# A recurrence and a routed mixture of experts in one kernel: another list of expert visits, other homes for the first raw weights, and new numbers in the planner

## The chip, the cores and the metric

The kernel runs on one core of one Trainium2 chip. The metric is device time in microseconds (us) of the slowest core, here of the only one. Three timed runs of the kernel before gave a median of 621.38 us (621.37 to 622.74). One more execution, of 622.83 us, was profiled; every row below is from it.

## The reference

A gated recurrence runs over 4 sequences of 5056 steps with 256 channels. Its 20,224 result rows go through a router: a row whose skip score is not positive is passed on as it is, every other row goes to one of 8 experts, a two-layer network with a hidden width of 1024.

```python
f = lower_bound + (1 - lower_bound) * sigmoid(f_logit)
for t in range(S):
    h = f[:, t] * h + (1 - f[:, t]) * x[:, t];  y[:, t] = h
x = y.reshape(B * S, D)
do = x @ w_skip > 0
logits = x[do] @ w_gate;  e_idx = argmax(logits);  gate_w = softmax(logits)[e_idx]
out[do] = x[do] + gate_w * (relu(x[do] @ w1[e_idx]) @ w2[e_idx])      # the other rows: out = x
```

With the inputs of the reference the experts 0 to 7 get 1150, 1630, 1047, 1244, 1259, 1255, 1392 and 937 rows; the other 10,310 are passed on.

## The kernel before, in words

The sequence is cut into 20 chunks (19 of 256 steps, one of 192), each worth 8 tiles of 128 rows (the last 6). A chunk is loaded by ACT's queue (`load_z`, `load_x`), goes through `tanh` and `affine` on ACT, `mixin` and eight `scan` instructions on DVE, is transposed to rows by PE (`turn_out`) and copied by ACT (`evict`). PE multiplies it with the router's weights (`score`), and DVE works out for each row the expert and a place in that expert's region of a table in memory (`route0` to `route3`, the last of which writes `posi`; `gates`). GpSimd then writes the rows to their places with one indirect DMA per tile (`send`, L485), 8 to a chunk.

The experts' work is done in visits. A visit (e, ns, m) takes ns tiles of expert e out of the table once the chunks up to m are in it. The list VISITS (L57) has 22 of them with 72 tiles. `window` (DVE) sets where a visit reads: at the next unread row, or, where the region does not yet hold ns tiles more, further back, so that it ends at the last row there; the rows read twice are masked. `fetch` (SP) loads the rows, `turn_in` (PE) transposes them, `x_hi` and `x_lo` (ACT, DVE) split them into two parts, PE does the first layer as three products (`first`, L610), ACT and DVE rectify and split the hidden values (`rect_hi`, `rect_lo`), PE does the second layer (`second`, L653), DVE weighs the result (`weigh`, L658), and GpSimd writes one tile per indirect DMA to the output (`put_out`, L662). Weights come half an expert at a time by SP (`load_w`, L534) into raw buffers and are split by ACT and DVE (`split_hi`, `split_lo`). The first three visits use raw weights in plain float32, without splits.

What the list does not cover is worked out on the chip when all chunks are routed (`list1` to `list4`): windows of 2 tiles and of 3 tiles. One of the former and two of the latter (SURE) are part of the program as three more visits with the expert in a register. If there are more, a loop at the program's end does them one after the other (L960 to L990); every engine reads the count `more` and branches over the loop if it is zero.

The order of the instructions on each engine is fixed before the program runs, by a planner (`Plan.run`): each job has a cost, a due time, jobs that it needs and slots that it takes from rings which stand for buffers; an engine takes the first job by due time that can start in the planner's account. MOVES shifts due times by name, chunk and visit. The chip then runs each engine's queue in that order, and an instruction at its head that waits holds up all behind it.

`hold` (L538) gives a raw weight its buffer ahead of the load, by a memset of one element on DVE; the memset waits until the readers of what was there before are done. The raw weights of the first three visits have the tags `w1h` and `w2h`, three buffers each.

Of the kernel before, what the change touches and what calls it, by code (L numbers as in the profile page):

```python
# [40 lines left out]
NEAR, FAR, TURN = 0.2, 1.1, 140.0  # L41
MOVES = {
    ("tanh", "early"): 4.3, ("evict", "early"): -2.8, ("send", "early"): -1.8, ("load_x", "chunk", 2): -8.4,
    ("gates", "chunk", 3): 3.1, ("scan", "chunk", 4): -4.5, ("score", "chunk", 4): 1.4, ("scan", "chunk", 5): 2.8,
    ("turn_out", "chunk", 5): -3.2, ("route1", "chunk", 5): 3.2, ("score", "chunk", 6): 1.3,
    ("affine", "chunk", 7): 8.9, ("scan", "chunk", 7): 2.6, ("route3", "chunk", 7): -5.7, ("chunk", 8): -4.1,
    ("scan", "late"): -5.1, ("score", "late"): 0.3, ("score_turn", "late"): -3.0, ("turn_out", "late"): 5.7,
    ("route0", "late"): -10.1, ("chunk", 11): -0.7, ("chunk", 15): -2.3, ("chunk", 16): -1.8,
    ("hold", "early"): 2.5, ("pass_over", "visit", 0): -3.8, ("put_out", "early"): 10.4, ("hold", "visit", 1): -5.6,
    ("rect_all", "visit", 1): -16.1, ("split_lo", "early"): -0.6, ("turn_in", "visit", 3): 4.2,  # L50
    ("first", "visit", 3): 2.0, ("rect_hi", "early"): 4.0, ("split_lo", "visit", 4): -5.3,
    ("split_lo", "visit", 5): -1.0, ("x_lo", "visit", 5): -6.8, ("window", "visit", 6): -11.7,
    ("x_lo", "visit", 6): -10.7, ("rect_lo", "late"): 1.4, ("rect_lo", "visit", 6): -6.9,
    ("second", "visit", 6): 5.5, ("weigh", "visit", 6): 0.4, ("visit", 7): 4.1,
# [198 lines left out]
def hgrn_moe(ctx, tc, z_d, x_d, lb_d, wr_d, w1_d, w2_d, out_d, disp_d):  # L253
# [518 lines left out]
    for n, v in enumerate(visits):  # L772
# [94 lines left out]
    for v, t in zip(visits, begin):  # L867
# [160 lines left out]
```

## Time and profile before

| | us |
|---|---|
| median of three timed runs | 621.38 |
| the profiled execution | 622.83 |
| its span, first to last instruction | 621.1 |
| PE busy in the span | 571.6 (92%) |
| DVE busy | 490.2 (79%) |
| ACT busy | 348.2 (56%) |
| POOL busy | 284.9 (46%) |

A row of the timeline has the start, the duration, the engine (SPq is SP's queue, which issues DMAs; PEld the loading of weights), the line of the kernel, the operation, the tiles written and read, and in brackets how long the engine had been idle before and what ended that. Starts of neighbours tell more than durations: the durations of instructions that follow each other overlap.

### The profile page before, as it was taken

What the parts mean: (1) busy time and instruction counts of PE and PEld (TensorE: products, weight loads), DVE (VectorE), ACT (ScalarE), POOL (GpSimd) and SP (SyncE); (2) the same over time, 40 slices, a digit from 0 to 9 for tenths busy, and PEclk for the clock granted to TensorE, in tenths of its full rate; (3) what the DMA queues carried; (4) which work ended last, traced back from release to release, by engine and by line L of the source; (5) the groups of instructions that cost most, each with busy time, mean ns of one, the idle gap of its engine ahead of it and who ended that gap; (6) DMA issues with size and microseconds to landing.
All of it is one profiled execution on the core that took longest, in us unless ns stands there. A gap on an engine that the chain in (4) does not pass through costs nothing.

```text
span 621.1 us, 11689 instructions
## 1 busy us (share of the span) xinstructions
PE 571.6 (92%) x4012; PEld 513.2 (83%) x4012; DVE 490.2 (79%) x1131; ACT 348.2 (56%) x518; POOL 284.9 (46%) x297
## 2 busy tenths in 40 slices
PE   2648999996999999999999999999999999999981
PEld 1327888996899988989898899889999999999971
DVE  5997999896999999999999998567964567466351
ACT  5865687873784856677666544535443445354140
POOL 2278677876027374563788556274320322022201
PEclk9767999997999999999999999999999999999976
DMA  8898999987786697796988755564543417444100
GB/s 319 343 394 323 400 415 411 349 281 284 260 333 246 249 377 291 276 311 253 345 320 292 244 175 181 163 225 178 197 145 128 130 37 247 130 149 148 59 5 24
DMA packets 40431, 149.64 MB, mean 241 GB/s; under 512 B 9332, under 2 KB 10507, under 8 KB 33328
## 3 DMA queue, kind: packets, MB, share of 16 engines
q1 hardware_dynamic: 22544, 86.91, 39.8%
q10 hardware_dynamic: 6304, 41.42, 17.9%
q0 software_dynamic: 11520, 20.52, 8.9%
q8 instruction: 33, 0.54, 0.3%
q14 instruction: 30, 0.25, 0.1%
HBM read 106.79 MB, written 53.23 MB: 258 GB/s over the span
## 4 chain that ended last, share of the span: by engine, by line
PE 67%; DMA 12%; ACT 1%; DVE 1%; issue 1%; POOL 1%; POOLq 0%; SPq 0%; DVEq 0%
PE po L653 30%; PE ph L610 29%; DMA out<-xin 8%; PE pt L403 3%; PE px L560 3%; PE pq L381 2%; DMA rw<-w 2%; DMA xin<-dispatched 1%; DMA dispatched<-rows,posi 1%; POOL dispatched L485 1%; PE pl L395 0%; DVE hl L629 0%; ACT hh L617 0%; ACT w2h L548 0%; ACT zt L356 0%
## 5 line engine op out<-in xcount | busy, mean ns | idle before, releaser
L485 POOL DMA_INDIRECT dispatched<-rows,posi x158 | 179.9, 1139 | 156.7 <-issue 36.1
L617 ACT ACTIVATE hh<-ph 128x512 fp32r<-128x512 f32 (+1 forms) x164 | 93.3, 572 | 159.4 <-PE ph L610 138.2
L653 PE MATMUL po<-w2h,hh 128*128 128x256 f32 x616 | 177.8, 289 | 0.0
L653 PE MATMUL po<-w2l,hh 128*128 128x256 f32 x616 | 175.1, 284 | 0.4 <-DVE w2l L553 0.4
L653 PE MATMUL po<-w2h,hl 128*128 128x256 f32 x616 | 172.7, 280 | 0.4 <-DVE hl L629 0.2
L662 POOL DMA_INDIRECT out<-xin x82 | 90.9, 1108 | 173.9 <-DVE xin L658 136.7
L629 DVE SCALAR_TENSOR_TENSOR hl<-ph,hh 128x512 fp32r<-128x512 f32 (+1 forms) x164 | 105.8, 650 | 63.9 <-ACT hh L617 63.0
L610 PE MATMUL ph<-xh,w1h 128*128 128x512 f32 (+2 forms) x368 | 133.9, 364 | 1.2 <-ACT w1h L548 1.2
L610 PE MATMUL ph<-xh,w1l 128*128 128x512 f32 (+2 forms) x368 | 132.4, 360 | 1.8 <-DVE w1l L553 1.8
L610 PE MATMUL ph<-xl,w1h 128*128 128x512 f32 (+2 forms) x368 | 132.6, 360 | 0.0
L653 PEld LDWEIGHTS po<-w2h,hh 128*128 128x128 f32 x616 | 116.5, 189 | 4.7 <-issue 2.1
L653 PEld LDWEIGHTS po<-w2h,hl 128*128 128x128 f32 x616 | 116.5, 189 | 2.9 <-DVE hl L629 1.0
L653 PEld LDWEIGHTS po<-w2l,hh 128*128 128x128 f32 x616 | 116.2, 189 | 0.6 <-DVE w2l L553 0.6
L373 DVE TENSOR_TENSOR_SCAN xt<-zt,xt 128x256 f32<-128x256 f32 (+1 forms) x160 | 108.7, 722 | 3.8 <-issue 3.2
L610 PEld LDWEIGHTS ph<-xl,w1h 128*128 128x128 f32 x368 | 70.6, 192 | 8.8
L610 PEld LDWEIGHTS ph<-xh,w1h 128*128 128x128 f32 x368 | 70.2, 191 | 8.9 <-issue 2.1
L610 PEld LDWEIGHTS ph<-xh,w1l 128*128 128x128 f32 x368 | 70.5, 192 | 7.7 <-DVE w1l L553 2.0
L403 PE MATMUL pt<-ident,xt 128*128 128x128 f32 x316 | 50.7, 295 | 16.8 <-DVE xt L373 15.5
L548 ACT ACTIVATE w2h<-rw 128x1024 fp32r<-128x1024 f32 x46 | 48.7, 1060 | 29.4 <-PE po L653 24.4
L553 DVE TENSOR_TENSOR w2l<-rw,w2h 128x1024 fp32r<-128x1024 f32 x46 | 55.9, 1215 | 7.8 <-ACT w2h L548 7.6
L403 PEld LDWEIGHTS pt<-ident,xt 128*128 128x128 f32 x316 | 39.0, 149 | 26.4 <-issue 12.9
L553 DVE TENSOR_TENSOR w1l<-rw,w1h 128x1024 fp32r<-128x1024 f32 x46 | 55.9, 1218 | 3.4 <-ACT w1h L548 3.3
(126 smaller groups left out, 629.9 us busy)
## 6 DMA issues: line engine op xcount, KB each, us to landing
rw<-w SPq DMA_DIRECT2D x92, 512.0 KB, 4.8
out<-rows SPq DMA_DIRECT2D x19, 1032.0 KB, 10.0
zt<-z ACTq DMA_DIRECT2D x18, 1024.0 KB, 9.1
xt<-x ACTq DMA_DIRECT2D x18, 1024.0 KB, 5.2
xin<-dispatched SPq DMA_DIRECT2D x13, 516.0 KB, 5.3
w1f<-w SPq DMA_DIRECT2D x6, 512.0 KB, 8.4
w2f<-w SPq DMA_DIRECT2D x6, 512.0 KB, 10.0
dispatched<-rows,posi POOLq DMA_INDIRECT x158, 6.1
```

What stands on the lines that cost most here:

```text
L373: V.tensor_tensor_scan(out=xt[:, k, sl], data0=zt[:, k, sl], data1=xt[:, k, sl], initial=first_h, op0=ALU.mult, op1=ALU.subtract)
L381: T.matmul(pq[g * GR:(g + 1) * GR], wq[:, k], xt[:, k, 2 * P * g:2 * P * (g + 1)], start=(k == 0), stop=(k == KD - 1))
L403: T.transpose(pt[:, s_, k * P:(k + 1) * P], xt[:, k, (2 * g + s_) * P:(2 * g + s_ + 1) * P], ident)
L485: si = G.indirect_dma_start(out=disp_d, out_offset=bass.IndirectOffsetOnAxis(ap=posi[:, j:j + 1], axis=0), in_=rows[:, j], in_offset=None, ...
L548: A.activation(hi, v["raw"][h, nm], AF.Copy)
L553: V.tensor_tensor(out=lo, in0=v["raw"][h, nm], in1=v["w"][nm, h][0], op=ALU.subtract)
L560: T.transpose(px[:, s_ * P:(s_ + 1) * P], xin[:, s_, k * P:(k + 1) * P], ident)
L610: T.matmul(ph[:, i], a[:, k, cs], b[:, k, :w], start=(n == 0), stop=(n == 5))
L617: A.activation(th, v["hid"][u], AF.Relu)
L629: V.scalar_tensor_tensor(out=tl, in0=ph, scalar=0.0, in1=th, op0=ALU.max, op1=ALU.subtract)
L653: T.matmul(v["po"][p][:, q], a[:, i, cs], b[:, c], start=(fb == 0 and n == 0 and q == 0), stop=(fb == NFB - 1 and n == len(pairs) - 1), sk ...
L662: oi = G.indirect_dma_start(out=out_d, out_offset=bass.IndirectOffsetOnAxis(ap=v["ids"][:, s, D:D + 1], axis=0), in_=v["xin"][:, s], in_of ...
```

## The change

The list has the same 22 visits' worth of tiles in another order: (0, 3, 8) becomes (0, 3, 10) and goes two visits later, (3, 4, 11) becomes (3, 4, 13), (4, 4, 18) becomes (4, 4, 17), (0, 4, 17) becomes (0, 4, 19). The raw weights of the three first visits go to three tags, `r{}` with 2 buffers, `{}l` and `{}h` with 3 each. The planner's costs change (`send` 1.28 to 1.42, `put_out` 1.36 to 1.42, among others), a ring for `sq` and an order among takers of `{}l` are added, and MOVES is replaced by a longer table. The memory's zeroed margin (`clear`) now waits for a memset on DVE.

```diff
-NEAR, FAR, TURN = 0.2, 1.1, 140.0
+NEAR, FAR, TURN = 0.1, 0.8, 140.0
 MOVES = {
-    ("tanh", "early"): 4.3, ("evict", "early"): -2.8, ("send", "early"): -1.8, ("load_x", "chunk", 2): -8.4,
...
+    ("load_z", "early"): 5.7, ("load_x", "chunk", 0): 10.5, ("affine", "early"): 14.3, ("scan", "chunk", 0): -12.3,
...
-VISITS = [(3, 1, 0), (2, 2, 1), (1, 2, 2), (0, 2, 3), (3, 2, 4), (5, 2, 5), (6, 4, 7), (0, 3, 8), (1, 3, 8), (4, 4, 9), (7, 4, 10), (3, 4, 11), (5, 4, 12), (6, 4, 13), (1, 4, 15), (2, 4, 16), (0, 4, 17), (4, 4, 18), (5, 4, 19), (1, 4, 19), (3, 3, 19), (7, 4, 19)]
+VISITS = [(3, 1, 0), (2, 2, 1), (1, 2, 2), (0, 2, 3), (3, 2, 4), (5, 2, 5), (6, 4, 7), (1, 3, 8), (4, 4, 9), (7, 4, 10), (0, 3, 10), (5, 4, 12), (3, 4, 13), (6, 4, 13), (1, 4, 15), (2, 4, 16), (4, 4, 17), (5, 4, 19), (0, 4, 19), (1, 4, 19), (3, 3, 19), (7, 4, 19)]
...
+    def late_clear():
+        V.memset(zero[0:1, 0:1], 0.0)
...
+    HOMES = (("r{}", 2), ("{}l", 3), ("{}h", 3))
...
         if v["whole"]:
-            r = sb.tile(shp, F32, name=nm + "f", tag=nm + "h", bufs=3)
+            tag, n = HOMES[v["i"] % 3]
+            r = sb.tile(shp, F32, name=nm + "f", tag=tag.format(nm), bufs=n)
...
-            J["clear"] = job("SP", 1.3, ready[0], clear, need=[J["scan", 0][0, 0]], kb=760)
+            n_ = job("DVE", .07, ready[0] - 18, late_clear, need=[J["scan", 0][1, 0]])
+            J["clear"] = job("SP", 1.3, ready[0] - 18, clear, need=[n_], kb=760)
...
-        s1 = job("ACT", .32, r - 20.2, score_out, c, need=[s0], uses=[s_p])
-        s2 = job("PE", .24, r - 20.2, score_turn, c, need=[s1], takes=[s_l])
+        s_q = new_slot("sq")
+        s1 = job("ACT", .32, r - 20.2, score_out, c, need=[s0], takes=[s_q], uses=[s_p])
+        s2 = job("PE", .24, r - 20.2, score_turn, c, need=[s1], takes=[s_l], uses=[s_q])
...
-        J["send", c] = [job("POOL", 1.28, r - 11 + j * 1.2, send, c, j, need=[r3, ga, nu], uses=[s_r, s_o], kb=74, lands=2.8)
+        J["send", c] = [job("POOL", 1.42, r - 11 + j * 1.2, send, c, j, need=[r3, ga, nu], uses=[s_r, s_o], kb=74, lands=2.8)
...
-                s_raw = new_slot(nm + "h") if whole else new_slot("r" + nm)
+                own = HOMES[v["i"] % 3][0].format(nm) if whole else "r" + nm
+                s_raw = new_slot(own)
...
-                lo = job("DVE", 1.21, use - 4, split_lo, v, h, nm, need=[hi], takes=[s_lo], uses=[s_raw, s_hi])
+                lo = job("DVE", 1.21, use - 4, split_lo, v, h, nm, need=[hi], takes=[s_lo], uses=[s_raw, s_hi],
+                         after=taker.get(nm + "l"))
+                taker[nm + "l"] = lo
...
-            job("POOL", 1.36, end + 1 + s_, put_out, v, s_, need=[ob] + [J["keep", c] for c in range(m + 1)],
+            job("POOL", 1.42, end + 1 + s_, put_out, v, s_, need=[ob] + [J["keep", c] for c in range(m + 1)],
```

The places where the order moves are shown as the compiled programs have them, with the lines of each kernel (L543 before is L577 after, L485 is L517, L662 is L696).

DVE around the first `mixin` of chunk 4 (`xt_471`), before; `w1f_629` is the fourth raw first-layer weight and takes the buffer of the first one, `w1f_245`, which visit 0 reads:

```order
L506 TENSOR_SCALAR mask_all_173<-seqf2_157,end_594 128x2
L508 TENSOR_SCALAR place_92<-end_594 128x1
L364 SCALAR_TENSOR_TENSOR xt_471<-zt_349,xt_471 128x1024
L543 MEMSET w1f_629 1x1
L373 SCALAR_TENSOR_TENSOR xt_471<-zt_349,xt_342,xt_471 128x256 x4
```

The same place after, where chunk 4 is `xt_462`; `w1f_589` and `w1f_591` are visit 2's, in buffers that nothing has used before:

```order
L541 TENSOR_SCALAR place_92<-end_568 128x1
L577 MEMSET w1f_589 1x1
L577 MEMSET w1f_591 1x1
L577 MEMSET w2f_594 1x1
L396 SCALAR_TENSOR_TENSOR xt_462<-zt_363,xt_462 128x1024 x2
```

The memsets stand at the same place, and what they wait for is no longer there.

GpSimd up to the writes of chunk 7, before (`rows_976` is chunk 5, `rows_1166` chunk 6, `rows_1326` chunk 7):

```order
L662 DMA out<-xin_617 20224x258
L476 COPY rows_976<-idv_130 128x8
L662 DMA out<-xin_617 20224x258
L485 DMA dispatched<-rows_976,posi_1145 165888x258 x7
L476 COPY rows_1166<-idv_130 128x8
L485 DMA dispatched<-rows_976,posi_1145 165888x258
L485 DMA dispatched<-rows_1166,posi_1280 165888x258 x7
L476 COPY rows_1326<-idv_130 128x8
L485 DMA dispatched<-rows_1166,posi_1280 165888x258
L662 DMA out<-xin_769 20224x258 x2
L485 DMA dispatched<-rows_1326,posi_1523 165888x258 x8
```

And after (`rows_950` is chunk 5, `rows_1082` chunk 6, `rows_1395` chunk 7, `xin_674` visit 1, `xin_854` visit 2):

```order
L517 DMA dispatched<-rows_950,posi_1030 165888x258
L696 DMA out<-xin_674 20224x258 x2
L517 DMA dispatched<-rows_950,posi_1030 165888x258 x2
L508 COPY rows_1082<-idv_130 128x8
L517 DMA dispatched<-rows_950,posi_1030 165888x258 x5
L517 DMA dispatched<-rows_1082,posi_1279 165888x258 x6
L508 COPY rows_1395<-idv_130 128x8
L517 DMA dispatched<-rows_1082,posi_1279 165888x258 x2
L517 DMA dispatched<-rows_1395,posi_1510 165888x258 x8
L696 DMA out<-xin_854 20224x258 x2
```

Two output writes (visit 2's) that stood ahead of chunk 7's stand behind them now: three are ahead in all, where there were five.

GpSimd's last rows are the same in both but for the line numbers; here they are after. The second write of the last visit that is not in a loop stands behind the end of both loops:

```order
L1002 ISA
L1002 UNCONDITIONAL_BRANCH
L999 UNCONDITIONAL_BRANCH
L999 ISA
L999 UNCONDITIONAL_BRANCH
L696 DMA out<-xin_7367 20224x258
L1056 UNCONDITIONAL_BRANCH
```

L1002 is the loop over windows of 3 tiles, L999 the branch around both loops, L1056 the end.

Farther on, the two orders are compared at the thirteenth visit, (5, 4, 12) before and (3, 4, 13) after, which both lists have behind 33 tiles. What stands ahead of its first `x_lo` on DVE, and ahead of its first first-layer product on PE, counted in the compiled programs (kinds that are not named stand there equally often, but for a few of under 0.1 us):

| engine, kind | before | after |
|---|---|---|
| DVE `mixin` | 32 | 33 |
| DVE `scan` | 127 | 128 |
| DVE chunks through `route0` to `gates` | 14 | 15 |
| DVE `split_lo` | 38 | 41 |
| PE transposes of `turn_out` | 224 | 240 |

## Rows read from the trace of the kernel before

**Rows 1.** The page's first part: busy time, share of the span and instructions of each engine.

```profile
PE 571.6 (92%) x4012; PEld 513.2 (83%) x4012; DVE 490.2 (79%) x1131; ACT 348.2 (56%) x518; POOL 284.9 (46%) x297
```

**Rows 2.** The engines' busy time in five stretches of the span; behind each stretch its length, then busy us and instructions of PE, PEld, DVE, ACT and POOL, the granted PE clock, the DMA engines' share and GB/s.

```profile
50.00:140.00 90.00, 89.28 (x668) 79.23 (x667) 81.29 (x207) 68.52 (x104) 67.23 (x64) 0.98 0.95 363
140.00:150.00 10.00, 5.02 (x30) 4.85 (x28) 4.22 (x10) 3.09 (x4) 5.97 (x7) 0.66 0.80 319
150.00:376.00 226.00, 226.00 (x1627) 203.34 (x1626) 217.70 (x453) 145.98 (x218) 121.00 (x107) 1.00 0.78 279
376.00:590.00 214.00, 214.00 (x1484) 199.22 (x1482) 135.77 (x303) 91.79 (x142) 64.31 (x62) 1.00 0.46 153
590.00:621.10 31.10, 15.22 (x97) 14.36 (x96) 9.59 (x16) 6.69 (x10) 2.92 (x3) 0.71 0.04 14
```

**Rows 3.** The last output writes on POOL (timeline), and ahead of them from DVE's timeline the last two weighings of the list's and the SURE visits.

```profile
588.22 0.48 DVE L658 SCALAR_TENSOR_TENSOR xin<-po,xin 128x256 f32<-128x256 f32 x1 [2.89 <-PE po L653]
589.64 0.48 DVE L658 SCALAR_TENSOR_TENSOR xin<-po,xin 128x256 f32<-128x256 f32 x1 [0.93 <-PE po L653]
...
588.98 0.97 POOL L662 DMA_INDIRECT out<-xin  x1 [3.34 <-DVE xin L658]
609.12 0.97 POOL L662 DMA_INDIRECT out<-xin  x1 [19.16 <-DVE xin L658]
...
616.41 0.97 POOL L662 DMA_INDIRECT out<-xin  x1 [5.04 <-issue]
```

**Rows 4.** The page's group of the output writes: count, busy us, mean ns of one, idle us ahead of them by releaser.

```profile
L662 POOL DMA_INDIRECT out<-xin x82 | 90.9, 1108 | 173.9 <-DVE xin L658 136.7 <-issue 20.3 <-DVE place L508 12.1
```

**Rows 5.** The sequencers' instructions of L961 (the branch on `more`) and L964 (the branch on one loop's count: taken into the loop of 2-tile windows first, around the loop of 3-tile windows then): count, shortest, median and longest in ns, start of the first and of the last.

```profile
L961 POOLq COMPARE_BRANCH  x2: 38/39/40, 589.3 to 615.4; - x2
...
L964 PEldq COMPARE_BRANCH  x2: 65/2050/4036, 588.5 to 614.7; - x2
L964 POOLq COMPARE_BRANCH  x2: 34/48/63, 589.8 to 614.4; - x2
...
L964 POOLq INC_SWDGE_SEM  x1: 733/733/733, 614.6 to 614.6; - x1
```

**Rows 6.** Timelines of SP's queue at the start (the zeroed margin, the first weights), and of DVE, PE and SP's queue around 50 us.

```profile
5.96 0.35 SPq L347 DMA_DIRECT2D dispatched<-zero  x1
17.64 9.24 SPq L534 DMA_DIRECT2D w1f<-w  x3
...
49.42 1.22 DVE L364 SCALAR_TENSOR_TENSOR xt<-zt,xt 128x1024 f32<-128x1024 f32 x1
53.85 0.75 DVE L373 TENSOR_TENSOR_SCAN xt<-zt,xt 128x256 f32<-128x256 f32 x1 [3.21 <-issue]
53.86 0.06 DVE L543 MEMSET w1f<- 1x1 f32 x1
...
50.18 3.62 PE L604 MATMUL ph<-xf,w1f 128*128 128x128 f32 x16
...
53.95 0.33 SPq L534 DMA_DIRECT2D w1f<-w  x1
```

**Rows 7.** Timelines of POOL, SP's queue, PE and DVE around the seventh visit, (6, 4, 7): the second of the two output writes ahead of chunk 7, the first and the last of that chunk's eight writes into the table, the visit's fetch, its transposes (PE's row before and some after), its first `x_lo`.

```profile
119.21 0.97 POOL L662 DMA_INDIRECT out<-xin  x1 [0.30 <-DVE place L508]
120.49 0.98 POOL L485 DMA_INDIRECT dispatched<-rows,posi  x1 [0.31 <-issue]
...
131.31 0.97 POOL L485 DMA_INDIRECT dispatched<-rows,posi  x1 [0.31 <-issue]
...
136.51 0.34 SPq L518 DMA_DIRECT2D xin<-dispatched  x1
...
140.20 0.28 PE L653 MATMUL po<-w2l,hh 128*128 128x256 f32 x1
145.46 1.94 PE L560 MATMUL px<-ident,xin 128*128 128x128 f32 x8 [4.98 <-DMA xin<-dispatched]
...
147.21 0.69 DVE L579 TENSOR_TENSOR xl<-px,xh 128x512 fp32r<-128x512 f32 x1 [5.33 <-ACT xh L573]
```

**Rows 8.** What one instruction takes where several of a kind follow each other (a merged row: start, total, count): DVE's `scan`, `mixin` and `split_lo`; the first and the last rows of `route0` with `route1`, and of `route3` with `gates`, of chunk 6; twelve transposes of PE as the chain of waits has them.

```profile
34.38 3.27 DVE L373 TENSOR_TENSOR_SCAN xt<-zt,xt 128x256 f32<-128x256 f32 x5
38.26 2.35 DVE L364 SCALAR_TENSOR_TENSOR xt<-zt,xt 128x1024 f32<-128x1024 f32 x2
148.67 2.35 DVE L553 TENSOR_TENSOR w1l<-rw,w1h 128x1024 fp32r<-128x1024 f32 x2
97.53 0.23 DVE L417 TENSOR_REDUCE mx<-pl 128x8 f32<-128x64 f32 x1 [0.30 <-PE pl L395]
99.01 0.31 DVE L441 TENSOR_TENSOR_SCAN pf<-reset,M 128x72 bf16<-128x72 f32 x1
100.54 0.14 DVE L456 TENSOR_TENSOR base<-carr,pr 128x9 f32<-128x9 f32 x1
101.91 0.20 DVE L472 RECIPROCAL rows<-sm 128x8 f32<-128x8 f32 x1
...
447.02 1.31 PE px L560 x12
```

**Rows 9.** Timelines of DVE and PE at the thirteenth visit: its second `x_lo`, and its first first-layer product.

```profile
294.50 0.66 DVE L579 TENSOR_TENSOR xl<-px,xh 128x512 fp32r<-128x512 f32 x1
...
296.92 0.39 PE L610 MATMUL ph<-xh,w1h 128*128 128x512 f32 x1
```

More of the change, by code (lines that the diff above doesn't have):

```diff
@@ L40 @@
 T0, FETCH, LAG = 55.0, 22.0, 3
-NEAR, FAR, TURN = 0.2, 1.1, 140.0
+NEAR, FAR, TURN = 0.1, 0.8, 140.0
 MOVES = {
-    ("tanh", "early"): 4.3, ("evict", "early"): -2.8, ("send", "early"): -1.8, ("load_x", "chunk", 2): -8.4,
[L44 to L54, printed above, removed]
@@ new lines @@
+    ("load_z", "early"): 5.7, ("load_x", "chunk", 0): 10.5, ("affine", "early"): 14.3, ("scan", "chunk", 0): -12.3,
+    ("turn_out", "early"): 1.9, ("route0", "chunk", 0): -22.6, ("route1", "chunk", 0): -12.6,
+    ("route2", "early"): -2.3, ("route3", "early"): -11.2, ("gates", "early"): 4.0, ("number", "early"): -5.1,
+    ("send", "early"): -3.5, ("chunk", 1): 6.8, ("load_x", "chunk", 1): 11.3, ("mixin", "chunk", 1): 18.5,
+    ("scan", "chunk", 1): -11.8, ("turn_out", "chunk", 1): -21.6, ("evict", "chunk", 1): -27.4,
@@ new lines @@
+    ("scan", "chunk", 8): -9.9, ("score_turn", "chunk", 8): -26.4, ("turn_out", "chunk", 8): 6.2,
+    ("route2", "chunk", 8): 6.9, ("send", "late"): 11.1, ("chunk", 9): -1.1, ("mixin", "late"): 7.3,
+    ("affine", "late"): 7.4, ("scan", "late"): 7.7, ("score", "late"): -5.2, ("score_turn", "late"): -2.5,
+    ("turn_out", "late"): -0.9, ("evict", "late"): 5.3, ("route0", "late"): 8.8, ("exps", "late"): 14.2,
+    ("route2", "late"): -4.0, ("route3", "late"): 7.5, ("load_z", "late"): 1.4, ("chunk", 10): 4.8,
@@ new lines @@
+    ("load_x", "late"): 19.5, ("chunk", 11): 5.9, ("chunk", 12): -14.8, ("chunk", 13): 3.2, ("chunk", 15): 8.4,
+    ("chunk", 16): -10.0, ("chunk", 19): 2.4, ("window", "early"): 3.9, ("visit", 0): 2.9,
+    ("window", "visit", 0): 7.4, ("hold", "early"): 7.2, ("turn_in", "early"): 12.0, ("x_all", "early"): -12.5,
+    ("first", "early"): -10.0, ("rect_all", "early"): 13.8, ("rect_all", "visit", 0): 12.0,
+    ("second", "early"): 6.6, ("pass_over", "early"): 10.9, ("visit", 1): -2.3, ("window", "visit", 1): 6.9,
@@ new lines @@
+    ("first", "visit", 1): -20.2, ("rect_all", "visit", 1): -9.8, ("visit", 2): 2.8, ("window", "visit", 2): 1.7,
+    ("hold", "visit", 2): -9.8, ("first", "visit", 2): 36.0, ("second", "visit", 2): -3.8,
+    ("pass_over", "visit", 2): 15.7, ("put_out", "visit", 2): 8.8, ("visit", 3): 2.3, ("hold", "visit", 3): 7.4,
+    ("split_hi", "visit", 3): 26.4, ("split_lo", "visit", 3): -6.1, ("first", "visit", 3): 10.1,
+    ("rect_hi", "early"): 13.3, ("rect_lo", "early"): -4.7, ("second", "visit", 3): 12.4,
@@ new lines @@
+    ("pass_over", "visit", 3): 5.6, ("visit", 4): 13.0, ("hold", "visit", 4): 10.2, ("split_hi", "visit", 4): -18.8,
+    ("split_lo", "visit", 4): 7.9, ("turn_in", "visit", 4): -9.5, ("x_hi", "visit", 4): 21.5,
+    ("rect_lo", "visit", 4): 13.1, ("second", "visit", 4): 10.3, ("pass_over", "visit", 4): -27.1,
+    ("visit", 5): 4.6, ("split_lo", "visit", 5): 4.3, ("rect_lo", "visit", 5): -5.6, ("second", "late"): 4.7,
+    ("weigh", "late"): -46.8, ("visit", 6): 7.9, ("split_lo", "visit", 6): -23.5, ("split_hi", "late"): -15.6,
@@ new lines @@
+    ("split_lo", "late"): -5.7, ("turn_in", "visit", 6): -7.7, ("first", "late"): 2.0, ("first", "visit", 6): -8.4,
+    ("rect_hi", "late"): 6.9, ("rect_lo", "late"): 7.6, ("rect_lo", "visit", 6): -7.0, ("second", "visit", 6): -5.3,
+    ("window", "late"): 18.0, ("turn_in", "late"): 0.5, ("x_lo", "late"): 7.0, ("visit", 8): 2.9,
+    ("visit", 9): -5.0, ("visit", 11): -1.9, ("visit", 12): 2.0, ("visit", 13): 7.1, ("visit", 14): 2.2,
+    ("visit", 15): -4.9, ("visit", 16): -9.0, ("visit", 18): 0.9, ("visit", 19): -4.4, ("visit", 20): -6.8,
@@ L55 @@
+    ("visit", 21): -9.4, ("visit", 23): 10.0, ("visit", 24): 23.1,
 }
```

19 lines of the change are left out of this document (14 added, 5 removed).

## The prediction

> **What bounds the kernel now.** I read the stretches of the span first, then the end, then the waits of PE and DVE ahead of 150 us. PE is busy for 92% of the span [rows 1]. By stretches, it is never idle from 150 to 590 us, at the full granted clock; DVE is busy for 217.7 of 226 us up to 376, and for 135.8 of 214 behind that [rows 2]. So from 150 to 590 there is no idle time to take out: PE's own work is the length of that stretch, and up to 376 us DVE is close behind it. Time can be won at the two ends, and lost where DVE, which has little to spare up to 376, is asked for something sooner.
>
> At the end the last weighing outside a loop starts at 589.64 and takes 0.48, which is 590.12; the write that belongs to it starts at 616.41, and between the two stand the two writes of a loop's pass [rows 3]. The output writes number 82 [rows 4], while the list has 72 tiles and the SURE visits 8: the loop did one window of 2 tiles. In that stretch PE is busy for half the time at a granted clock of 0.71 [rows 2], because one visit alone has nothing to overlap with.
>
> At the start two waits stand out. DVE sits idle for 3.21 us ahead of 53.85 with "issue" as releaser; right there its queue has the memset of `w1f_629`, which takes the buffer that visit 0 is reading, and PE's products of visit 0 run from 50.18 to 53.80; the load behind that memset is issued at 53.95 [rows 6]. And visit 6 comes too soon for its rows: PE idles 4.98 us and DVE 5.33 [rows 7].
>
> **Part 1, the list.** A visit takes rows from the next unread one, so what is left can be counted from the reference's inputs. Before, expert 0 has 261 rows by chunk 3 and 256 are read. At chunk 8 it has 502, so (0, 3, 8) must step back by 138 to find 3 tiles. With 4 tiles more 1014 of its 1150 rows are read, and 136 rows, two tiles, are left. Expert 2 leaves 347, expert 4 235, expert 6 368: two windows of 2 and two of 3, one more of 2 than SURE has. After, (0, 3, 10) finds 708 rows and steps back by nothing, (0, 4, 19) ends with the last row, and nothing is left of expert 0. The rest is one window of 2 and two of 3, what SURE covers: 80 tiles and no pass of a loop. Experts 3 and 5, whose visits move too, are read to their last row in both.
>
> The price: GpSimd branches around both loops instead of into one. Before, it read the count early and branched at 589.3 [rows 5]. What then stands between it and the last write is what stood there when it branched around the second loop: branch at 614.4, a semaphore step of 0.73, write at 616.41, 2.0 us in all [rows 3, 5]. So the write starts at 589.3 + 2.0 = 591.3, later than the 590.12 of its data. From 616.41 to 591.3 is 25.1 us. What follows that write, 621.1 - 616.41 = 4.7 us, stays.
>
> A long branch can cost more: PE's, around the body of the second loop, took 4036 ns against 65 for the one that fell into the first, and GpSimd's never more than 63 [rows 5]. The Trainium skill (Runtime: NRT & Kernel Launch, section Instruction fetch mechanics) says that a taken branch whose target lies outside the instructions fetched ahead stalls until they are fetched. PE's row agrees with it, and GpSimd's row shows that its code around one loop is short enough; by the page GpSimd might stall around both. PE branches at 588.5 [rows 5] and with 4.04 is through near 592.5, ahead of the end at 596, so that is covered. For GpSimd I take nothing, and keep 4.04 as the upper bound.
>
> **Part 2, the homes.** The first three visits' raw weights no longer share three buffers, and the memsets ahead of chunk 4 take buffers that nothing has used. The 3.21 us go. Not all of it need come through: bounds 0 and 3.2; I take 3.2, since no other reader stands there. Visit 2's four loads can be issued some us sooner, in a stretch where the DMA engines are busy 95% [rows 2]; that is the bound below: a chunk's loads pushed back by 1.5 MB at 363 GB/s, 4 us, if nothing of it were hidden.
>
> **Part 3, visit 6.** Its fetch starts at 136.51, after chunk 7's writes; those start at 120.49, right behind two output writes. In the new order these stand behind chunk 7. From one write's start to the next is 1.28 (119.21 to 120.49), so chunk 7 can be in the table 2.6 us sooner and the rows at 142.7 instead of 145.3. PE was ready for them at 140.5, so some 2 us of its wait stay. Behind the long wait the granted clock was 0.66 [rows 2], the lower of its two levels for a time, and eight transposes took 1.94 us where twelve take 1.31 at the full clock [rows 7, 8]: 1.1 us more than they need. Behind 50 to 140 us of short waits it was 0.98 [rows 2], so I let the shorter wait keep the full clock. DVE's wait shrinks by 2.6 + 1.1 = 3.7. Bounds: 0, and 5.3.
>
> **Part 4, the price in the middle.** The new list wants chunks sooner, and DVE has to make them ahead of the same visits. At the thirteenth visit, behind 33 tiles in both, DVE has done one chunk and three splits more, and one scan: `mixin` 2.35/2 = 1.2; routing 99.01 + 0.31 - 97.53 and 101.91 + 0.20 - 100.54, 3.4; `scan` 3.27/5 = 0.65; three `split_lo` at 2.35/2, 3.5 [rows 8]; 8.8 in all. PE has 16 transposes more, 16 x 1.31/12 = 1.7 [rows 8]. Before, `x_lo` ended at 295.16 and its visit began at 296.92: 1.8 to spare [rows 9]. So DVE is late by 8.8 - 1.7 - 1.8 = 5.3 if it recovers nothing. It recovers 3.2 (part 2) and 3.7 (part 3), together 6.9: the visit can begin 1.6 us sooner than before, and no more, whatever PE gained. PE then has the same tiles left as before, and DVE has room from 376 us on [rows 2]. So the part ahead of the loop ends 1.6 us sooner.
>
> **The rest.** The zeros for the table's margin go out after four scans of chunk 0, near 12 us instead of 5.96; SP's next are the weights at 17.64 [rows 6], so nothing is queued behind them, and the table is read tens of us later. The load order z, z, x, x changes which half comes second; the first `mixin` needs a z half through ACT anyway. The ring for `sq` and the takers change order only. Nothing for these; 1 us either way.
>
> **Sum.** 25.1 + 1.6 = 26.7 off the profiled execution's 622.83 (span 621.1 and 1.7 around it), 596.1. That execution lies 1.45 above the median of 621.38; on the median's scale 594.7 us.
>
> **Rivals.**
> (a) DVE recovers nothing: the waits it loses come back elsewhere, as other waits at its queue's head. For it: DVE is busy 81 of 90 us from 50 to 140 and DMA 95% [rows 2]. Against: the wait at 53.85 had a cause that is removed. Time: 621.4 - 25.1 + 5.3 = 601.6.
> (b) GpSimd's branch stalls like PE's: 594.7 + 4.0 = 598.7. Against it the 63 ns of its own branch.
> (c) Better than forecast: visit 6 waits for nothing, its slow clock goes, and DVE's counts do not bind because it loses less in small waits than before: PE's 4.98 and 1.1 for the 1.6, so 594.7 + 1.6 - 6.1 = 590.2.
> (d) The loop still runs, so that the change does not do what it says: 621.4 - 1.6 = 619.8. For it only a miscount; the 82 writes bear out the same count before.
> (e) Slower than before: rows come late for many visits. Visits 7 to 15 now want their chunk's writes with DVE and GpSimd some us from the edge. If each waited as visit 6 did, 4.98 for the rows and 1.1 at the slow clock, 6.1 per visit; five such visits eat the 26.7 and it is slower from there, and all nine give 594.7 + 55 = 650. For it: the counts of part 4 are tight, and an order that is good in an account can be bad on the chip. Against: before, only visit 6 waited so; PE has no gap behind it until 590 [rows 2].
>
> **How the numbers follow.** Forecast, with its own range of 590 to 600, 0.55; (a) 0.16; (b) 0.08; (c) 0.10; (d) 0.03; (e) or some of its waits without the whole 0.08, half of it over 621. The range that holds the time 8 times in 10 is 588.5 to 604. A difference under 0.3% (1.9 us) can't be told from none: faster 0.94, same 0.02, slower 0.04.
>
> **What would show it.** Output writes number 80, and no row of a loop's body is there; the last write starts within 2 us of its weighing. DVE's idle time ahead of chunk 4's scans is gone. Visit 6's transposes wait under 2 us for rows. At the thirteenth visit `x_lo` ends less than a us ahead of PE's first product, or PE waits for it. I am wrong in part 4 if PE idles over 5 us in all between 150 and 590, in part 1 if the last write is over 3 us behind its weighing, and in the whole if the loop's lines are in the trace.

## The result, and the profile after

The changed kernel takes 604.28 us in the median of 4 runs (600.68 to 605.55), where the kernel before takes 621.38: a ratio of 0.9718, with a 95% interval of 0.9667 to 0.9769. Faster it is, but by 17.1 us where 26.7 were forecast, and 604.28 lies 0.28 above the range. The profiled execution took 603.43 us against 622.83 before, 19.4 less; it lies 0.85 below its own median, as before's lies 1.45 above, so on the forecast's own scale 7.3 us are missing.

The page's first part and its group of the output writes, which answer to [rows 1, 4]:

```profile
PE 556.0 (92%) x3912; PEld 496.0 (82%) x3912; DVE 481.2 (80%) x1117; ACT 339.3 (56%) x508; POOL 283.3 (47%) x295
...
L696 POOL DMA_INDIRECT out<-xin x80 | 92.8, 1160 | 168.6 <-DVE xin L692 147.9
```

There are 80 writes, and no row of a loop's body. Now the end, in the timelines of DVE and POOL, which answer to [rows 3]:

```profile
593.62 0.48 DVE L692 SCALAR_TENSOR_TENSOR xin<-po,xin 128x256 f32<-128x256 f32 x1 [2.86 <-PE po L687]
595.03 0.48 DVE L692 SCALAR_TENSOR_TENSOR xin<-po,xin 128x256 f32<-128x256 f32 x1 [0.93 <-PE po L687]
...
594.38 0.97 POOL L696 DMA_INDIRECT out<-xin  x1 [6.72 <-DVE xin L692]
596.72 0.97 POOL L696 DMA_INDIRECT out<-xin  x1 [1.37 <-DVEq L999]
```

The last weighing ends at 595.51 and the last write starts 1.21 behind it. So the end is as forecast (1.2), and what is missing lies ahead of it: the weighing should have ended at 588.5, 1.6 sooner than before's 590.12, and ends 5.39 later.

The stretches show from where. Behind each its length, then busy us and instructions of PE, PEld, DVE, ACT and POOL, the granted PE clock, the DMA engines' share and GB/s; the rows answer to [rows 2]:

```profile
20.00:50.00 30.00, 18.85 (x102) 10.82 (x104) 28.59 (x80) 18.94 (x28) 17.76 (x18) 0.57 1.01 387
50.00:140.00 90.00, 79.19 (x581) 68.10 (x574) 78.78 (x204) 64.27 (x100) 65.28 (x62) 0.99 0.95 362
140.00:150.00 10.00, 10.00 (x87) 10.00 (x87) 9.89 (x14) 8.68 (x12) 5.77 (x6) 1.00 0.96 332
150.00:376.00 226.00, 223.16 (x1611) 198.97 (x1610) 215.05 (x454) 140.44 (x213) 128.40 (x115) 1.00 0.78 278
sum 356.00, PE 331.20 PEld 287.89 DVE 332.31 ACT 232.33 POOL 217.21; mean PE 82.80 PEld 71.97 DVE 83.08 ACT 58.08 POOL 54.30
```

The same sum of the kernel before, which was not shown yet:

```profile
sum 356.00, PE 336.82 PEld 296.16 DVE 331.90 ACT 237.23 POOL 213.51; mean PE 84.20 PEld 74.04 DVE 82.98 ACT 59.31 POOL 53.38
```

The seventh visit's wait is gone: from 140 to 150 us PE is busy throughout, where it was for 5.02 us. But from 50 to 140 it lost 10.1 us, and behind 150 another 2.8. Up to 376 us PE has been busy for 5.6 us less than before, and from there to 575 us neither kernel lets it idle: that is about the 5.39. DVE was idle for 356 - 331.90 = 24.1 us before and for 23.7 now. The forecast had it win back 6.9 us of its idle time; it won back 0.4.

That balance has two halves. The stretches up to 150 us and from there to the thirteenth visit, first of the kernel before and then of the changed one:

```profile
20.00:150.00 130.00, 110.82 (x776) 92.82 (x776) 114.20 (x303) 91.25 (x136) 92.51 (x88) 0.88 0.94 359
150.00:305.00 155.00, 155.00 (x1116) 140.42 (x1115) 149.56 (x310) 104.10 (x153) 75.20 (x68) 1.00 0.80 291
```

```profile
20.00:150.00 130.00, 108.04 (x764) 88.92 (x763) 117.26 (x296) 91.89 (x138) 88.81 (x84) 0.89 0.96 365
150.00:305.00 155.00, 152.16 (x1104) 137.33 (x1103) 146.41 (x307) 99.54 (x149) 87.87 (x77) 1.00 0.82 297
```

Up to 150 us DVE is idle for 12.7 us where it was for 15.8: it won back 3.1. From 150 to 305 us it is idle for 8.6 us where it was for 5.4, and the 3.1 are gone again. Nearly all of that is the length of one wait, in the timelines of ACT and DVE:

```profile
263.97 1.06 ACT L388 ACTIVATE zt<-zt 128x1024 f32<-128x1024 f32 x1 [3.35 <-DMA zt<-z]
...
266.38 0.56 DVE L663 SCALAR_TENSOR_TENSOR hl<-ph,hh 128x384 fp32r<-128x384 f32 x1 [3.07 <-ACT hh L651]
```

The `hh` for which DVE waits stands in ACT's queue behind a `zt` that waits 3.35 us for its load.

### The profile page after: what moved, and what is told of

Same layout as the page of the kernel before. It is cut to its first block, busy times and chain, and to the rows that moved or that the text cites. A ratio compares the mean times of both kernels' runs of the same rounds, so it can differ in the third digit from the quotient of the medians.

```text
span 601.6 us, 11330 instructions
## 1 busy us (share of the span) xinstructions
PE 556.0 (92%) x3912; PEld 496.0 (82%) x3912; DVE 481.2 (80%) x1117; ACT 339.3 (56%) x508; POOL 283.3 (47%) x295
## 4 chain that ended last, share of the span: by engine, by line
PE 64%; DMA 11%; DVE 5%; ACT 2%; issue 2%; POOL 1%; POOLq 0%; SPq 0%; DVEq 0%; ACTq 0%
PE po L687 28%; PE ph L644 28%; DMA out<-xin 4%; DMA dispatched<-rows,posi 3%; PE pt L435 3%; PE px L594 2%; DMA xin<-dispatched 2%; PE pq L413 2%; POOL dispatched L517 1%; DVE xt L405 1%; DMA rw<-w 1%; DMA out<-rows 1%; DVE w2l L587 1%; DVE hl L663 1%; PE ph L638 1%
## 5 line engine op out<-in xcount | busy, mean ns | idle before, releaser
L517 POOL DMA_INDIRECT dispatched<-rows,posi x158 | 177.4, 1123 | 144.2 <-issue 35.8
L696 POOL DMA_INDIRECT out<-xin x80 | 92.8, 1160 | 168.6 <-DVE xin L692 147.9
L687 PE MATMUL po<-w2h,hh 128*128 128x256 f32 x600 | 171.9, 286 | 0.0
L687 PE MATMUL po<-w2l,hh 128*128 128x256 f32 x600 | 168.9, 281 | 0.0
L687 PE MATMUL po<-w2h,hl 128*128 128x256 f32 x600 | 168.2, 280 | 0.0
L644 PE MATMUL ph<-xh,w1h 128*128 128x512 f32 (+2 forms) x352 | 130.5, 371 | 1.3 <-DVE hl L663 1.3
L644 PE MATMUL ph<-xl,w1h 128*128 128x512 f32 (+2 forms) x352 | 127.1, 361 | 0.0
L644 PE MATMUL ph<-xh,w1l 128*128 128x512 f32 (+2 forms) x352 | 126.6, 360 | 0.0
L687 PEld LDWEIGHTS po<-w2h,hl 128*128 128x128 f32 x600 | 113.1, 189 | 2.5
L644 PEld LDWEIGHTS ph<-xh,w1h 128*128 128x128 f32 x352 | 66.1, 188 | 10.1 <-issue 3.4
L644 PEld LDWEIGHTS ph<-xl,w1h 128*128 128x128 f32 x352 | 66.1, 188 | 9.1
L644 PEld LDWEIGHTS ph<-xh,w1l 128*128 128x128 f32 x352 | 66.4, 189 | 5.4
```

The lines of the kernel that those rows point to most:

```text
L517: si = G.indirect_dma_start(out=disp_d, out_offset=bass.IndirectOffsetOnAxis(ap=posi[:, j:j + 1], axis=0), in_=rows[:, j], in_offset=None, ...
L644: T.matmul(ph[:, i], a[:, k, cs], b[:, k, :w], start=(n == 0), stop=(n == 5))
L687: T.matmul(v["po"][p][:, q], a[:, i, cs], b[:, c], start=(fb == 0 and n == 0 and q == 0), stop=(fb == NFB - 1 and n == len(pairs) - 1), sk ...
L696: oi = G.indirect_dma_start(out=out_d, out_offset=bass.IndirectOffsetOnAxis(ap=v["ids"][:, s, D:D + 1], axis=0), in_=v["xin"][:, s], in_of ...
```

## The experiments

Two theories at first. **R**: the order of the head (ahead of 150 us) lets raw weights land late; ACT and DVE stand behind them and PE idles. **L**: the new list asks more of DVE than any head can make up for. What speaks for R is the table of DVE's waits from 8 to 150 us (waiting instruction, what it waited for: us in total, times, longest), and one such wait in the timelines of SP's queue, ACT and DVE:

```profile
DVE w1l L587 <- ACT w1h L582: 4.6, 3, 2.1
DVE w2l L587 <- ACT w2h L582: 2.4, 1, 2.4
...
62.76 0.90 SPq L567 DMA_DIRECT2D rw<-w  x2
...
74.26 1.06 ACT L582 ACTIVATE w1h<-rw 128x1024 fp32r<-128x1024 f32 x1 [4.34 <-DMA rw<-w]
...
75.35 1.22 DVE L587 TENSOR_TENSOR w1l<-rw,w1h 128x1024 fp32r<-128x1024 f32 x1 [1.84 <-ACT w1h L582]
```

The load issued at 62.76 releases ACT at 74.26, and DVE's `split_lo` stands right behind ACT's split: 7.0 us of DVE's time go into such waits. The first four kernels:

**e1, the list alone.** The edit in the kernel before, whose order stays word for word up to the seventh visit:

```
-VISITS = [ ... (6, 4, 7), (0, 3, 8), (1, 3, 8), (4, 4, 9), ...
+VISITS = [ ... (6, 4, 7), (1, 3, 8), (4, 4, 9), (7, 4, 10), (0, 3, 10), ...
```

> The kernel before with the new list of visits alone; the order up to the seventh visit is before's, word for word. Theory R (the 7 us missing come from the head, ahead of 150 us: raw weights that land late and hold ACT and DVE, so that PE idles): the head is before's, PE idles about 6 us ahead of 150 as before, the loop's 25.1 us go, and at most part 4's price of 5.3 us is paid in the middle: 596 to 602 us. Theory L (the new list itself asks DVE for too much in the middle, whatever the head does): PE idles over 8 us between 150 and 590, and the time is 604 us or more.

Measured: 606.37 us, ratio 0.9748 (0.9714 to 0.9781). The interval overlaps the changed kernel's: the homes, the new table and the new costs together can't be told from nothing beside the list. R's 596 to 602 fell. Of L's two numbers the time came, the idle time did not (PE idles 4.2 us from 150 to 376 and none from there to 575). Up to 150 us PE loses next to nothing (busy for 110.6 us from 20 on, for 110.8 before), so this kernel loses behind 150 us, where the changed one loses half ahead of it. What does show is the chain of waits (start, us, what): between 249 and 297 us it runs on DVE alone; the end of that, and what follows, are

```profile
296.28 0.67 DVE xt L373
296.97 8.63 DMA zt<-z
305.62 1.06 ACT zt L356
306.68 0.97 ACT xh L573 x2
```

And at the thirteenth visit, in the timelines of DVE and PE:

```profile
307.20 1.29 DVE L579 TENSOR_TENSOR xl<-px,xh 128x512 fp32r<-128x512 f32 x2
...
307.98 0.44 PE L395 MATMUL pl<-ident,sq 128*128 128x128 f32 x2 [0.66 <-ACT sq L388]
...
308.61 0.48 PE L610 MATMUL ph<-xh,w1h 128*128 128x512 f32 x1
```

`x_lo` ends at 308.49 and PE's first product follows 0.12 behind it; before it was 1.76 [rows 9]. So with this list DVE has nothing to spare, as part 4 has it, and the visit begins 11.7 us later than before's 296.92. But what comes after DVE in the chain is a load and ACT, and the 0.66 us that PE stands idle here are put down to ACT's `sq`: that PE waits for `x_lo` itself is not shown.

**e2, the loop alone.**

```
-SURE = ((0, 1), (1, 2))
+SURE = ((0, 2), (1, 2))
```

> The kernel before with SURE = ((0, 2), (1, 2)): the same 82 tiles, the last window of two tiles as a visit of the list and no pass of the loop. If part 1 is right that what the loop costs is that one visit alone overlaps with nothing, two tiles in the steady stretch cost about 2 x 5.7 = 11.4 us of PE and the other 13.7 of the 25.1 go: 607 to 609 us. Rival: the 25.1 us are the tiles' own work and the end's fixed steps, and the loop itself is nearly free: 617 to 621 us.

Measured: 609.78 us, ratio 0.9806 (0.9778 to 0.9835); 11.7 us by the medians, 14.2 by the profiled executions (608.65 against 622.83), with the forecast's 13.7 between; 609.78 lies 0.78 above the range that was named. Running two tiles in a loop rather than in the list costs about as much as the 11.4 us that the tiles themselves were estimated at. Part 1 holds.

**e3 and e4, what the table of moves brings.** e3 is the kernel before with the new list and the homes (the planner knows of them); e4 is the changed kernel with before's `NEAR, FAR` and `MOVES`:

```
-NEAR, FAR, TURN = 0.1, 0.8, 140.0
+NEAR, FAR, TURN = 0.2, 1.1, 140.0
...
-    ("load_z", "early"): 5.7, ("load_x", "chunk", 0): 10.5, ...
+    ("tanh", "early"): 4.3, ("evict", "early"): -2.8, ...
```

> The kernel before with the new list and the three homes; the table of moves, NEAR and FAR, and the costs of the scatters as before, so that the planner makes an order of its own. Theory R: the weights of the first visits go out earlier, as in the changed kernel, and the waits of ACT for raw weights ahead of 150 us grow over before's 3 us; 599 to 606 us. Theory L: no better than e1. If the homes are worth their 3.2 us, it is 3 us faster than e1.

> The changed kernel with before's table of moves, NEAR and FAR; list, homes, zeros, load order and costs as changed. It tells what the new table is worth. Theory R: ACT's waits for raw weights ahead of 150 us are a matter of the order that the table sets, so they are other than the 13.4 us of the changed kernel, and the time goes with PE's idle time up to 150 us, one for one: 598 to 612 us. Theory L: PE's idle time lies behind 150 us, and the time is above 604 us.

Measured: e3 610.33 us, ratio 0.9793 (0.9743 to 0.9843); e4 612.53 us, ratio 0.985 (0.9821 to 0.988). Both lie above R's ranges. The homes are not worth 3 us in e3, it is slower than e1, though in an order of the planner's own; the new table is worth some 8 us to a kernel that has the rest of the change. ACT's waits for raw weights up to 150 us are 9.1 us in e3 and 5.7 in e4, less than the changed kernel's 13.4, and both kernels are slower: against R. What grew is DVE's wait for `hh` (10.6 and 13.9 us up to 376), and DVE's idle time as a whole, to 32.4 and 31.6 us.

So I formed two others. **D**: DVE's own work, in the order in which it stands, sets the time up to the thirteenth visit, and a wait that is taken away there comes back under another name. **B**: the head is bound by its transfers. e5 and e6 cut each chunk's dense write to 64 of a row's 258 columns (the 1032 of the expectation are a row's bytes), in the changed kernel and in the one before:

```
-        wi = SP.dma_start(out_d[...].rearrange(...), st[c]["rows"][:, :nt])
+        wi = SP.dma_start(out_d[...].rearrange(...)[:, :, 0:64], st[c]["rows"][:, :nt, 0:64])
```

> The changed kernel, with each dense write of a chunk's rows to the output cut to 64 of its 1032 columns (the rest of those rows is left out of the output). The order of every engine is the changed kernel's, row for row; only the transfers are lighter, by half a megabyte and more a chunk. Theory R (raw weights land late because the DMA engines are full, and ACT and DVE stand behind them): ACT's waits for raw weights ahead of 150 us fall from about 15 us to under 6, PE's stalls between 60 and 140 us shrink by 5 us or more, and the time falls to 594 to 599 us. Theory D (DVE's own work and the order it is in are the limit, whatever the transfers do: what DVE does not wait for weights it waits for something else): 601 to 604 us.

> The control: the kernel before with the same cut of the dense writes, order unchanged. Theory R: before's raw weights hold ACT up by only 3 us ahead of 150 us, and the wait of visit 6 for its rows hangs on GpSimd's order, so little is won: 618 to 621 us, clearly less than in e5. Theory D: the same as e5's gain, within 1 us, and both small.

Measured: e5 609.58 us, ratio 0.9814 (0.9758 to 0.987); e6 621.78 us, 1.0008 (0.9977 to 1.0038). e5 lies above both theories' ranges, and it did not test what it was for: the cut rows made packets smaller but more of them, as the page's DMA line shows, first of the changed kernel and then of e5:

```profile
DMA packets 39615, 147.28 MB, mean 245 GB/s; under 512 B 9159, under 2 KB 10333, under 8 KB 32512
```

```profile
DMA packets 57279, 131.58 MB, mean 217 GB/s; under 512 B 29383, under 2 KB 30557, under 8 KB 52608
```

From 50 to 140 us the DMA engines' share went from 0.95 only to 0.90. ACT's waits for raw weights were 10.4 us, and `sq` held PE for 7.2. Inconclusive for B.

**e7, part 2 by itself.** The buffers of the three homes in the kernel before, and the planner's account left as it was, so that no instruction moves:

```
-            r = sb.tile(shp, F32, name=nm + "f", tag=nm + "h", bufs=3)
+            tag, n = HOMES[v["i"] % 3]
+            r = sb.tile(shp, F32, name=nm + "f", tag=tag.format(nm), bufs=n)
```

> The kernel before with the three homes as buffers only, the planner's account left as it was, so that every engine's order is before's, row for row. It is part 2 of the change by itself. By part 2 DVE's wait of 3.21 us ahead of 53.85 us goes and comes through: 618.2 us. Rival (a), that DVE recovers nothing because other waits take its place at the queue's head: the wait goes and DVE's idle time between 20 and 376 us stays at 24 us, within 1.5; 620.5 to 622 us.

Measured: 622.37 us, ratio 1.0009 (0.9986 to 1.0032). This is the cleanest of the runs. DVE's timeline at the place of [rows 6], and its waits from 20 to 376 us:

```profile
50.68 0.06 DVE L545 MEMSET w1f<- 1x1 f32 x1
50.77 0.75 DVE L373 TENSOR_TENSOR_SCAN xt<-zt,xt 128x256 f32<-128x256 f32 x1
...
54.96 0.22 DVE L417 TENSOR_REDUCE mx<-pl 128x8 f32<-128x64 f32 x1 [1.51 <-PE pl L395]
...
71.04 0.23 DVE L417 TENSOR_REDUCE mx<-pl 128x8 f32<-128x64 f32 x1 [2.87 <-PE pl L395]
```

```profile
DVE xl L581 <- ACT xh L575: 6.8, 3, 6.4
DVE mx L417 <- PE pl L395: 5.4, 5, 2.9
```

The wait of 3.21 us is gone: the scan starts at 50.77, 3.1 us sooner than before. At 54.96 and at 71.04 DVE waits for a chunk's scores instead, 4.4 us in all, and at the seventh visit for 6.4 us where it was 5.33. Its idle time from 20 to 376 us is 25.3 us, no less than before's 24.1. So in before's order part 2's gain is zero, and rival (a)'s mechanism is shown there: what was won at 50 us is lost again by 72. The time alone would not tell, since with the old list PE is busy for 225.5 of the 226 us behind 150 whatever DVE wins. With the new list the homes were not tried in an order that stays.

**e8, raw weights sooner.**

```
-SOON = {0: 25, 1: 20, 2: 10, 3: 5}
+SOON = {0: 25, 1: 20, 2: 10, 3: 10, 4: 8}
```

> The changed kernel with SOON = {..., 3: 10, 4: 8}: the loads of visit 3's and 4's raw weights are due 5 and 8 us earlier; the planner makes a new order from some 60 rows on. Theory R: ACT's waits for raw weights shrink by several us, and the time goes down by 2 to 5 us, to 599 to 602. Theory D: no change beyond a reshuffle's 2 us either way, and the waits of DVE come back with other names.

Measured: 607.11 us, ratio 0.9775 (0.9727 to 0.9822). DVE's waits for the splits up to 376 us fall from 8.4 to 3.7 us, its idle time stays (23.6), other waits fill it, and the time does not go down: not R's 599 to 602. It lies 2.8 us above the changed kernel's by the medians, a little more than D allowed, in an order that the planner made anew; the intervals overlap.

**e9 to e12, lighter transfers and lighter work.** The dense write cut to 16 of 128 partitions in the changed kernel (e9, e12) and in the one before (e10); the weighing cut to 32 of 256 columns (e11):

```
-        wi = SP.dma_start(out_d[...].rearrange(...), st[c]["rows"][:, :nt])
+        wi = SP.dma_start(out_d[...].rearrange(...)[0:16], st[c]["rows"][0:16, :nt])
```

> The changed kernel with each dense write of a chunk's rows to the output cut to 16 of its 128 partitions (the other rows are left out of the output): packets as large as before and an eighth of them, where e5 had as many packets, only shorter. Order of every engine unchanged. About 0.93 MB a chunk less, some 7 MB and 20 us of transfer at 362 GB/s ahead of 150 us. Theory B (the head is bound by its transfers: the engines' waits move from one to another, and none of them can be won by moving instructions): ACT's waits for raw weights shrink below 6 us, PE's stalls between 60 and 140 us fall by 5 us or more, and the time to 592 to 598 us. Theory D (DVE's own work and order are the limit): 601 to 604 us.

> The same cut in the kernel before, order unchanged. Theory B: before is bound by its transfers in the head as well, so it wins about what it stalls there that the order does not need, 5 to 10 us: 612 to 617 us. If only the changed kernel's raw weights were late: 619 to 622 us. Theory D: 620 to 622 us.

> The changed kernel with each weighing on DVE cut to 32 of 256 columns (the rest of the product is left out of the output), order unchanged: 80 weighings of 0.476 us become some 0.2 to 0.3, so DVE has 4 us less to do up to 150 us and 6 to 9 less from 150 to 376. Theory D: DVE's work is what PE waits for, and the time falls by as much as PE idles from 150 to 376 us and more, 3 to 7 us: 597 to 601. Theory B: the head, which the transfers bind, keeps its stalls, and only the middle's 3 us can go: 601 to 604 us.

> The kernel of e9 once more, the order of the changed kernel with an eighth of the dense writes: e9 to e11 ran on a chip on which the kernel before takes 661.6 us and engines pause where the trace names no releaser, and the changed kernel did not run beside them. Where the kernel before takes some 621.5 us: theory B (what the changed kernel lost hangs on late transfers, of raw weights ahead of 150 us and of a visit's rows near 198): ACT's waits for raw weights ahead of 150 us fall below 6 us, the 10.37 us of the fetch at 188.3 fall to about 4, PE's stalls between 60 and 140 us fall by 5 us or more, and the time is 592 to 598 us, a ratio of 0.953 to 0.962. Theory D (DVE's work and order set it, and a wait that goes comes back under another name): 601 to 605 us, a ratio of 0.967 to 0.974.

Measured, each beside the kernel before on its chip: e9 634.94 us, ratio 0.9535 (0.9459 to 0.9612); e10 667.0 us, 1.0116 (1.0051 to 1.0181); e11 640.49 us, 0.9691 (0.9644 to 0.9738); e12 630.62 us, 0.9582 (0.9523 to 0.9642). Beside them the kernel before takes 661 us, 40 more than in all other sessions, on two chips; one of the two is the chip of e5 to e8 by its number, and there it took 621.8, so this need not be a property of the chip. e9's and e12's ratios lie below the changed kernel's 0.9718, as B has it; but e10, the control, went the other way from B's 612 to 617, and the changed kernel was not run beside them. ACT's waits put down to raw weights did shrink (2.4 and 2.3 us), but so they did in e11 (2.3), whose transfers are the changed kernel's: pauses of the kind in the last section came in, and they can have done it. So whether lighter transfers would give the missing time back is open, and so is e11's question: its interval overlaps the changed kernel's.

**An account over the runs.** It was made afterwards, so no expectation holds it. Take for each kernel 622.83 (or, with the new list, 603.03, which is rival (a)'s sum on the profiled execution's scale: 622.83 - 25.1 + 5.3), and add what DVE idles from 20 to 376 us over before's 24.1:

| kernel | DVE idle, us | by the account | profiled execution |
|---|---|---|---|
| changed | 23.7 | 602.6 | 603.43 |
| e1 | 27.0 | 606.0 | 606.21 |
| e3 | 32.4 | 611.3 | 611.76 |
| e4 | 31.6 | 610.5 | 611.48 |
| e5 | 27.5 | 606.4 | 608.13 |
| e6 (old list) | 21.4 | 620.1 | 620.95 |
| e7 (old list) | 25.3 | 624.0 | 624.47 |
| e8 | 23.6 | 602.5 | 606.81 |

Seven of eight come out 0.2 to 1.7 us above the account. e8 does not (4.3): there the thirteenth visit's first product stands 2.3 us behind its `x_lo`, so PE and not DVE was last, as it was by 1.04 in the changed kernel. This is agreement over orders, not a run that changes DVE's idle time alone; and what holds up PE, ACT or a load leaves DVE idle too, so the account does not say which of them is the cause.

## Why the prediction was right, and where it was wrong

**Part 1, right.** 80 writes, no loop, the last write 1.21 us behind its weighing. e2 bears out the price of the loop, 11.7 to 14.2 for 13.7. GpSimd's branch did not stall, which settles rival (b). The sequencers' branches on `more`, as their line's rows have them (count, shortest/median/longest ns, start):

```profile
L999 PEldq COMPARE_BRANCH  x1: 3446/3446/3446, 593.3 to 593.3; - x1
L999 POOLq COMPARE_BRANCH  x1: 45/45/45, 594.7 to 594.7; - x1
L999 POOLq INC_SWDGE_SEM  x1: 689/689/689, 595.2 to 595.2; - x1
```

PE's 3.4 us are covered, as forecast: it is through at 596.7, ahead of the end at 601.6. What the Trainium skill (Runtime: NRT & Kernel Launch, section Instruction fetch mechanics) says of a taken branch that leaves the fetched instructions agrees with PE's row; by it GpSimd might have stalled as well, and its 45 ns show that it did not.

**Part 2, wrong.** "I take 3.2, since no other reader stands there": in e7 the wait went, and DVE's idle time did not (25.3 us for 24.1). There the bound of zero was the answer: the removed wait moved up what stood behind it in DVE's queue, and that had to wait for PE's scores.

**Part 3, wrong in its mechanism, though its sign came.** "Chunk 7 can be in the table 2.6 us sooner": the two output writes do stand behind chunk 7 now, in POOL's timeline (first of its eight writes, and the output write that follows the last), with the visit's fetch and transposes on SP's queue and PE:

```profile
120.92 1.18 POOL L517 DMA_INDIRECT dispatched<-rows,posi  x1 [2.91 <-ACT zt L388]
133.46 0.97 POOL L696 DMA_INDIRECT out<-xin  x1 [0.30 <-DVE xin L692]
...
140.08 0.34 SPq L551 DMA_DIRECT2D xin<-dispatched  x1
...
147.71 1.04 PE L594 MATMUL px<-ident,xin 128*128 128x128 f32 x8
```

But the chunk's first write starts at 120.92, not sooner than before's 120.49, behind 2.91 us in which GpSimd stood idle. The write needs the places of chunk 7, and DVE had them at 119.62, where it had them at 113.60 before; the bracket names ACT's `zt`, so what ended the wait last, and why DVE came 6.0 us later, stays open. The fetch goes out at 140.08, 3.6 us later than before's 136.51 [rows 7]. PE does not wait for it because PE itself comes later, at 147.71. The wait of 4.98 us was not won; PE loses 10.1 us to small waits between 50 and 140 us. The longest three kinds of them (what it waited for: us in total, times, longest):

```profile
PE pl L427 <- ACT sq L420: 2.5, 2, 2.0
PE px L594 <- DMA xin<-dispatched: 2.0, 2, 1.2
PE pr L480 <- DVE pf L473: 1.7, 1, 1.7
```

In all, 5.2 us are put down to ACT, 3.7 to DVE and 2.0 to fetches: no single cause.

**Part 4, right in the price, wrong in what pays for it and in how it reaches PE.** The step that failed is "It recovers 3.2 (part 2) and 3.7 (part 3), together 6.9": by 150 us 3.1 had come back, and by 305 us nothing was left of it, DVE being busy for 263.7 of 285 us as before (263.8). DVE's and PE's rows at the thirteenth visit, which answer to [rows 9]:

```profile
302.25 1.28 DVE L613 TENSOR_TENSOR xl<-px,xh 128x512 fp32r<-128x512 f32 x2
...
304.45 0.28 PE L687 MATMUL po<-w2l,hh 128*128 128x256 f32 x1
304.57 0.40 PE L644 MATMUL ph<-xh,w1h 128*128 128x512 f32 x1
```

`x_lo` ends at 303.53, 8.4 us later than before's 295.16, where the counts of DVE's additional work said 8.8: DVE recovered 0.4. But it ends 1.04 ahead of PE's product, just outside the "less than a us" that was named, and PE runs its second-layer products one behind the other up to that product: it was not held by `x_lo`. PE was late already. The product is 7.65 later than before; less the 1.7 us of transposes that PE has done by then, 5.95 should come through, and the weighing at the end is 5.39 late. PE was late by 2.8 us at 150, and the other 2.84 came at 155 us (1.31, for DVE's `hl`), at 198 (0.86, for the rows of a fetch) and at 266 to 268 (0.66). My sign for being wrong here, PE idling over 5 us behind 150, did not show: half of the loss lay ahead of 150, where the sign does not reach.

**Rival (a) comes nearest**: 25.1 gained, 5.39 lost for its 5.3, and next to nothing recovered. Its sum on the profiled execution's scale is 603.03 and 603.43 was measured; on the median's 601.6 and 604.28. That its 5.3 agree so well is in part luck, since they were worked out for a PE that waits for `x_lo` at the thirteenth visit, and PE did not. I gave it 0.16, though its reason stood in [rows 2]: DVE busy for 81 of 90 us and the DMA engines at 95%, which may leave no room into which the work that a wait held back could be moved. Whether it is DVE's own work and order or the transfers that take the room is not settled (e9 to e12). The range's upper end was too low by 0.28.

**The rest** cost nothing that shows: the first visit's transposes start at 53.1 us for 48.9, but PE does chunks' work meanwhile and is busy for 2.3 us more from 20 to 50 us than before. Part 2's bound of 4 us counts 1.5 MB, but four loads of 512 KB are 2.1 MB, 5.8 us at the same rate; the sum does not use it.

## What to carry to other kernels

A wait at the head of an engine's queue is worth its length only if what stands behind it is ready; before counting it, read what the next ten instructions wait for, and sum the engine's idle time over the whole stretch rather than wait by wait. Work that an engine must do sooner is a price that can be counted from the order (8.8 counted, 8.4 measured); idle time that it is to win back in a stretch where it is 90% busy is not a credit until a run has shown it. And a lateness that is counted on one engine has to be followed to the engine that sets the time: here the count came true, and the engine that it was to hold up was late already.

## What the runs showed of the hardware

Two tiles in the pass of a loop cost 11.7 us more than in the list, by the medians of e2. Of the engines that branch around the loops' body only PE pays for it, 3446 ns against 45 on GpSimd, 54 on ACT and 72 on DVE; in e1 to e5 and e8 PE's branch takes 3365 to 3726.

Fewer bytes in shorter packets need not be lighter transfers: in e5 16 MB less in 45% more packets left the DMA engines' share between 50 and 140 us at 0.90 for 0.95.

In e9 to e12 engines paused together where the same instructions did not pause elsewhere. In e12, ACT's and DVE's timelines:

```profile
62.19 0.60 ACT L656 ACTIVATE hf<-ph 128x512 f32<-128x512 f32 x1 [5.22 <-remote]
...
62.23 0.17 DVE L488 TENSOR_TENSOR base<-carr,pr 128x9 f32<-128x9 f32 x1 [6.01 <-remote]
```

The two wait for different products of PE, both of which have rows that end by 56.9, and resume within 0.04 us of each other; ACT pauses for 5.17 us at the same instruction in e11, on another chip, and not in the changed kernel's own trace. The trace names no releaser, and the cause is open.
